# Linear attention on one core: GpSimd adds the seven odd tiles of phi of k, takes relu of k in one piece, and scatters two heads of the output

## The chip, the core and the metric

The kernel runs on one core of a Trainium2 chip. The core has five engines that run beside each other: TensorE (PE in the profile; its weight loads are listed apart as PEld), VectorE (DVE), ScalarE (ACT), GpSimd (POOL) and SyncE (SP, which here only issues transfers). Sixteen DMA engines move data between the chip's memory (HBM) and the core's SBUF. The metric is the time of one execution on the device in microseconds (us); lower is better.

## The reference

The inputs q, k and v have the shape (1, 32, 2048, 128): 32 heads of 2048 rows of 128 numbers in bf16. It is attention without a softmax, so nothing is quadratic in the number of rows.

```python
phi_q = jnp.where(q > 0, q + 1, jnp.exp(q)) + 1e-6
phi_k = jnp.where(k > 0, k + 1, jnp.exp(k)) + 1e-6
kv  = jnp.einsum("bhsd,bhse->bhde", phi_k, v)        # 128 x 128 a head
z   = jnp.einsum("bhsd->bhd", phi_k)                 # column sums
num = jnp.einsum("bhqd,bhde->bhqe", phi_q, kv)
den = jnp.einsum("bhqd,bhd->bhq", phi_q, z)[..., None] + 1e-6
return num / den
```

The kernel uses that phi(x) = min(exp(x), 1) + 1e-6 + relu(x). It never needs the sum of the two parts in one tensor: a matmul with the first part (called `emk` or `emq`) and one with the second (`rk` or `rq`) that accumulate into the same place do the addition. Where the sum is formed first, one matmul takes the place of two.

## The kernel before

**Layout.** A head of q, k, v or the output is 128 partitions of 16 tiles of 128 columns, 4 KB a partition and 512 KB in all. Six buffers each hold heads of k, v and q, ten hold heads of the output.

**What a head goes through.** SP loads k, v and q (L380). ACT makes exp of k (L387). DVE makes `emk` = min(exp, 1) + 1e-6 (L401), 2048 columns at once. POOL makes `rk` = relu of k (L391): heads 0 and 2 in one piece of 2048 columns, head 1 on DVE, heads from 3 on in two halves of 1024. POOL then adds `emk` to `rk` in place for some tiles (L409). PE multiplies these with v (L432) into `kvz_ps`, and for some tiles a matmul of one column with a vector of ones (L339) gives z. For the odd tiles z comes for nothing from a column of ones in v, which POOL writes over the last column of the even tiles of v (memset, L445) once PE has read these. ACT copies `kvz_ps` to SBUF (L449). PE transposes q (L455); ACT makes exp of it (L466) and relu of its second half (L473); DVE makes relu of its first half (L475, source in PSUM) and `emq` (L487), 2048 columns at once. PE makes numerator and denominator of five groups of tiles (L502 with `emq`, L503 with `rq`); DVE adds 1e-6 to the denominators (L525), inverts them (L531) and multiplies (L536 for the last tile, L543 for the rest, in two pieces: groups 0 and 1, then 2 to 4). SP stores the head (L590).

**Which tiles are added.** `ADD` lists the tiles for which POOL forms the sum. For heads from 2 on these are 10 to 14, a block of 640 columns. For the tiles of `ADD`, PE does one matmul; for the others two, one with `emk` and one with `rk`. PE takes the even tiles first, those that need both parts (`both_of`) and then those of `ADD` (`one_of`), in an operation of its own that waits for the add (L442); after that, in the next turn, the odd tiles (`kv2`, L447), which wait for the add and the column of ones.

**Order.** Every operation has a key, and each engine runs its operations in the order of their keys; waits on semaphores follow from what each reads and writes. The keys are heads plus a fraction. On POOL the keys h - 0.45 (first half of relu), h (second half), h + 0.5 (add) and h + 0.6 (memset) give this order:

```
add(h-1), relu(h) first half, memset(h-1), relu(h) second half, add(h), relu(h+1) first half, memset(h), ...
```

The add of head h waits, beside its data, for `emq` of head h - 1 on DVE (`more=`, L421). On DVE a turn is: L525, L531, L536, L543 twice for head n, L475 for n + 2, L401 for n + 3, L487 for n + 2. On PE: num of head n, groups 0 and 1, the odd tiles of n + 1, num of head n, groups 2 to 4, the transposes of n + 2, the even tiles of n + 2.

**Stores.** SP issues all loads and stores in one order; a store's key (`late`, 1 + 1.18 h) puts the later stores behind the last loads. One head, 28, is in `SLOW`: POOL stores it after all its other work with an indirect transfer (L597), a scatter whose row numbers come from seven small DVE instructions at the start (L327 to L334). The row numbers of partitions 16 to 19 and 48 to 51 are out of bounds there, so those rows are left out of the scatter, and SP stores them in four small transfers of 3, 1, 3 and 1 partitions. The last head goes out in two stores.

The functions that the change touches, with the line numbers of the profile:

Of the kernel before, what the change touches and what calls it, by code (L numbers as in the profile page):

```python
# [12 lines left out]
def _ap(base: bass.AP, elem_offset: int, dims):  # L13
    return bass.AP(base.tensor, base.offset + elem_offset, [list(base.ap[0])] + [list(d) for d in dims])
# [217 lines left out]
def bass_standalone__linear_attn_elu__prompt_kernel(  # L232
# [16 lines left out]
    NG = 7  # L249
    HALF = NT * P // 2  # L250
    LAST = NH - 1
    SLOW = {LAST - 3: (16, 48)}

    ADD = (10, 11, 12, 13, 14)
    EVEN, ODD = tuple(range(0, NT, 2)), tuple(range(1, NT, 2))
    MORE = (4, 6, 8, 10, 12, 14)
    GAP = 32
# [7 lines left out]
    with ExitStack() as es:  # L265
        def sb(name, shape, dt):
            return es.enter_context(nc.sbuf_tensor(name, shape, dt))
# [17 lines left out]
        part_sb = sb("part_sb", [P, 1], mybir.dt.int32)  # L285
        off_sb = sb("off_sb", [P, len(SLOW)], fp32)
        num_sb = sb("num_sb", [P, len(SLOW)], fp32)
        row_sb = sb("row_sb", [P, len(SLOW)], mybir.dt.int32)

# [10 lines left out]

        for n, c in (("k", NBI), ("q", NBI), ("v", NBI), ("va", 1), ("o", NBO + 1 + len(SLOW))):
            for i in range(c):
                dsems[(n, i)] = es.enter_context(nc.semaphore(f"s_{n}{i}"))

        pl = Plan()

        def rows(x, h):
# [11 lines left out]
                                                     base=0, pattern=[[-1, P]], channel_multiplier=1),  # L319
               reads=[("id0",)], writes=[("ident",)])  # L320
        pl.add("pool", -7, lambda g: g.memset(_ap(vfull, 0, [[VW, NBI], [1, GAP]]), 1.0), writes=[("vones",)])

        pl.add("pool", -6.9, lambda g: g.iota(part_sb[:], pattern=[[0, 1]], base=0, channel_multiplier=1), writes=[("part",)])
        for i, (h, groups) in enumerate(SLOW.items()):
            off, num, row = off_sb[:, i:i + 1], num_sb[:, i:i + 1], row_sb[:, i:i + 1]
# [12 lines left out]
        def mm_held(pe, out_ap, rhs, stop, start=False):  # L338
            return pe.add_instruction(mybir.InstMatmult(  # L339
                start_tensor_calc=start, stop_tensor_calc=stop, ldweights=False, bass_skip_group_check=True,  # L340
                tile_position=(0, 0), tile_size=(P, P), name=nc.get_next_instruction_name(), engine=mybir.EngineType.PE,
                ins=[pe.lower_ap(rhs), pe.lower_ap(held[0])], outs=[pe.lower_ap(out_ap)]))
# [27 lines left out]
        for h in range(NH):  # L370
            def at(name, key, h=h):
                return place.get((name, h), h + key)

            bi, b2, b3, bo = h % NBI, h % 2, h % 3, h % NBO

            def load(name, buf, src, key, h=h, bi=bi):
                dst, rws = buf[:, bi], rows(src, h)
                if name == "v":
# [9 lines left out]
                   reads=[("k", bi)], writes=[("ek", b2)])  # L388
            def relu_k(eng, key, parts, h=h, bi=bi, b3=b3):
                c = slice(parts[0] * HALF, (parts[-1] + 1) * HALF)  # L390
                pl.add(eng, key, lambda e: e.tensor_scalar(rk_sb[:, b3, c], k_sb[:, bi, c], BIG, 0.0, op0=ALU.min, op1=ALU.max),  # L391
                       reads=[("k", bi)] + ([("rk", h - 1, 1)] if 0 < h < 3 else []),
                       writes=[(n, b3, p) for p in parts for n in ("rk", "rkx")] + [("phik", b3), ("phix", b3)], kind="rk")

            if h < 3:
                relu_k("dve" if h == 1 else "pool", at("rk", 0), (0, 1))
            else:
                relu_k("pool", h - 0.45, (0,))
                relu_k("pool", h, (1,))
            pl.add("dve", at("emk", -3 + 0.95),  # L400
                   lambda d, b2=b2, b3=b3: d.tensor_scalar(emk_sb[:, b3, :], ek_sb[:, b2, :], 1.0, EPS, op0=ALU.min, op1=ALU.add),  # L401
                   reads=[("ek", b2)], writes=[("emk", b3)], kind="emk")

            def add(eng, key, tiles, name, b3=b3, more=()):
                step = tiles[1] - tiles[0]

                def f(e):
                    a, b = (_ap(x[:, :, :], b3 * NT * D + tiles[0] * D, [[step * D, len(tiles)], [1, D]]) for x in (rk_sb, emk_sb))
                    return e.tensor_tensor(out=a, in0=a, in1=b, op=ALU.add)  # L409
                pl.add(eng, key, f, reads=[("emk", b3), ("rkx", b3, 0), ("rkx", b3, 1)] + list(more), writes=[(name, b3)], kind=name)  # L410

            if h == 0:
                add("dve", -2.04, range(NT), "phik")
                both_of, one_of = (), range(NT)
            elif h == 1:
                add("dve", -1.89, MORE, "phix")
                add("dve", -1.88, tuple(j for j in ADD if j in ODD), "phik")
                both_of, one_of = tuple(j for j in EVEN if j not in MORE), MORE
            else:
                add("pool", h + 0.5, ADD, "phik",  # L420
                    more=[("emq", (h - 1) % 3)] + ([("phik", 1)] if h == 2 else []))  # L421
                both_of, one_of = (tuple(j for j in EVEN if (j in ADD) == x) for x in (False, True))

            def kv(pe, tiles, start=False, stop=False, h=h, bi=bi, b3=b3, both_of=both_of):
                for j in tiles:
                    both = j in both_of or (j in ODD and j not in ADD and h > 0)
                    for src in (emk_sb, rk_sb) if both else (rk_sb,):
                        first, fin = start and j == tiles[0] and src is (emk_sb if both else rk_sb), stop and j == tiles[-1] and src is rk_sb
                        w = src[:, b3, j * D:(j + 1) * D]
                        l = j == 0 or (j in ODD and h > 0)  # L430
                        c = GAP + j * D
                        last = pe.matmul(kvz_ps[:, 1 - l:NC], lhsT=w, rhs=v_sb[:, bi, c - l:c + D], start=first, stop=fin,  # L432
                                         skip_group_check=True)
                        if not l:
                            held[0] = w
                            last = mm_held(pe, kvz_ps[:, 0:1], ones_sb[:, 0:1], fin)
                return last
            base = [("v", bi), ("vo", bi), ("ones",), ("vones",)]
            if h:
                pl.add("pe", at("kv", -1.2), lambda pe, kv=kv, t=both_of: kv(pe, t, start=True),  # L440
                       reads=[("emk", b3), ("rk", b3, 0), ("rk", b3, 1)] + base, writes=[("bankkv",)])
            pl.add("pe", at("kv", -1.199), lambda pe, kv=kv, t=one_of, f=h == 0: kv(pe, t, start=f, stop=f),  # L442
                   reads=[("phix" if h == 1 else "phik", b3)] + base + ([] if h else [("first",)]), writes=[("bankkv",)])
            if h:
                pl.add("pool", h + 0.6, lambda g, bi=bi: g.memset(_ap(vfull, bi * VW + GAP + D - 1, [[2 * D, NT // 2], [1, 1]]), 1.0),  # L445
                       reads=[("v", bi)], writes=[("vo", bi)], kind="vo")
                pl.add("pe", at("kv2", -0.2985), lambda pe, kv=kv: kv(pe, ODD, stop=True),  # L447
                       reads=[("phik", b3), ("emk", b3), ("rk", b3, 0), ("rk", b3, 1), ("v", bi), ("vo", bi)], writes=[("bankkv",)])
            pl.add("act", at("kvs", -0.95), lambda a, b3=b3: a.activation(kvs_sb[:, b3, :], kvz_ps[:, 0:NC], ACT.Copy),  # L449
                   reads=[("bankkv",)], writes=[("kvs", b3)], kind="kvs")  # L450
# [31 lines left out]
            else:  # L482
# [5 lines left out]
                   reads=[("eq", b2, 0), ("eq", b2, 1)], writes=[("emq", b3)], kind="emq")  # L488
# [105 lines left out]
            late = h + 1.0 + 0.18 * h  # L594
            if h in SLOW:
                i = list(SLOW).index(h)
# [3 lines left out]
                    reads=[("row", i)] + [("o", bo, p) for p in ("t", 0, 1, 2, 3, 4)], dma=("o", NBO + 1 + i))  # L600
# [38 lines left out]
```

## Time and profile before

| | |
|---|---|
| median of 3 runs | 167.63 us (167.09 to 167.91) |
| the profiled execution: time | 167.01 us |
| the profiled execution: span from first to last instruction | 165.7 us |
| granted clock of TensorE | 1.00 |
| moved by DMA | 67.25 MB, 406 GB/s over the span |
| add on POOL (L409), 640 columns | 30 times, 1397 ns |
| relu on POOL (L391), 1024 columns | 58 times, 1041 ns |
| relu on POOL (L391), 2048 columns | 2 times, 1894 ns |
| emk on DVE (L401) | 32 times, 688 ns |
| emq on DVE (L487) | 32 times, 691 ns |
| scatter on POOL (L597) | once, 1138 ns |

How to read it: the page gives the busy time of each engine as a share of the span, then the span in 40 slices with a digit for the busy tenths, then the chain of work that ended last, followed back from the last instruction. The timeline lists single instructions as start, duration, engine, line, operation, tensors; brackets behind it hold the idle time before it and what ended that. The waits list who waited for whom: total, times, longest. Starts on DVE lie up to 0.09 us before the end of the instruction ahead, since an instruction begins while its forerunner drains; so the price of an instruction is best read from start to start.

### The profile page before, as it was taken

How to read it: one execution, taken by the hardware profiler on the slowest of the kernel's cores; microseconds unless marked ns; L12 is line 12 of the kernel's file. 1: busy time of each engine (PE TensorE's matmuls, PEld its weight loads, DVE VectorE, ACT ScalarE, POOL GpSimd, SP SyncE). 2: the span in 40 equal slices, each digit the busy share in tenths (PEclk: the TensorE clock that was granted, in tenths of full speed). 3: DMA queues.
4: the chain of work that ended last, by engine and by line, in shares of the span. 5: the costliest groups of instructions: out<-in, count | busy, mean ns of one | idle time of the engine just before them, and what ended most of it. 6: DMA issues, size and time to landing. Idle time of an engine off the chain costs nothing.

```text
span 165.7 us, 6280 instructions
## 1 busy us (share of the span) xinstructions
PE 156.2 (94%) x2819; PEld 145.5 (88%) x2453; DVE 153.6 (93%) x277; ACT 155.2 (94%) x143; POOL 107.6 (65%) x130
## 2 busy tenths in 40 slices
PE   7779999999999999999999999999999999999990
PEld 0359899999999999999999989999998999999980
DVE  3587999999999999999999999999999999999993
ACT  3979999999999999999999999999999999999693
POOL 2405787676768867676787767677876767788320
PEclk9999999999999999999999999999999999999999
DMA  5999999999999999999999999999999999999986
GB/s 195 363 419 417 415 415 419 411 411 412 419 420 418 419 419 417 422 418 419 417 421 418 419 420 414 424 416 422 417 421 418 419 419 419 424 415 422 414 344 272
DMA packets 18605, 67.25 MB, mean 406 GB/s; under 512 B 2082, under 2 KB 2210, under 8 KB 18594
## 3 DMA queue, kind: packets, MB, share of 16 engines
q1 hardware_dynamic: 18448, 66.63, 99.2%
q0 software_dynamic: 144, 0.49, 0.7%
q8 instruction: 5, 0.08, 0.2%
q14 instruction: 6, 0.05, 0.1%
q10 hardware_dynamic: 2, 0.00, 0.0%
HBM read 50.33 MB, written 16.81 MB: 405 GB/s over the span
## 4 chain that ended last, share of the span: by engine, by line
DVE 62%; PE 16%; POOL 12%; DMA 4%; issue 3%; ACT 1%; SPq 1%; DVEq 0%
DVE o_sb L543 21%; POOL rk_sb L409 12%; DVE rq_sb L475 12%; DVE emq_sb L487 10%; DVE emk_sb L401 10%; PE kvz_ps L432 6%; PE o_ps L502 5%; PE o_ps L503 5%; DMA k_sb<-in_k_dram 4%; DVE rden_sb L531 3%; DVE o_sb L536 3%; DVE den_sb L525 2%; ACT ek_sb L387 1%; SPq L380 1%; DVE rk_sb L409 0%
## 5 line engine op out<-in xcount | busy, mean ns | idle before, releaser
L432 PE MATMUL kvz_ps<-v_sb,rk_sb 128*128 128x129 bf16 (+1 forms) x512 | 67.0, 220 | 2.7 <-POOL rk_sb L409 0.8
L543 DVE TENSOR_TENSOR o_sb<-o_ps,rden_sb 128x768 bf16<-128x768 f32 (+2 forms) x62 | 67.8, 1134 | 0.0
L409 POOL TENSOR_TENSOR rk_sb<-rk_sb,emk_sb 128x640 bf16<-128x640 bf16 x30 | 41.9, 1397 | 39.4 <-DVE emq_sb L487 38.1
L391 POOL TENSOR_SCALAR rk_sb<-k_sb 128x1024 bf16<-128x1024 bf16 (+1 forms) x60 | 64.2, 1070 | 2.4 <-DMA k_sb<-in_k_dram 2.4
L502 PE MATMUL o_ps<-kvs_sb,emq_sb 128*128 128x129 bf16 (+1 forms) x536 | 65.2, 217 | 0.0
L503 PE MATMUL o_ps<-kvs_sb,rq_sb 128*128 128x129 bf16 (+1 forms) x536 | 64.4, 217 | 0.0
L387 ACT ACTIVATE ek_sb<-k_sb 128x2048 bf16<-128x2048 bf16 x32 | 61.0, 1907 | 2.6 <-DMA k_sb<-in_k_dram 2.6
L466 ACT ACTIVATE eq_sb<-xT_ps 128x2048 bf16<-128x2048 bf16 (+1 forms) x33 | 60.0, 1822 | 2.1 <-PE xT_ps L455 2.1
L432 PE MATMUL kvz_ps<-v_sb,emk_sb 128*128 128x129 bf16 (+1 forms) x338 | 53.3, 221 | 0.5 <-DVE emk_sb L401 0.3
L432 PEld LDWEIGHTS kvz_ps<-v_sb,rk_sb 128*128 128x128 bf16 x512 | 46.1, 98 | 7.5 <-POOL rk_sb L409 2.7
L502 PEld LDWEIGHTS o_ps<-kvs_sb,emq_sb 128*128 128x128 bf16 x536 | 51.2, 98 | 0.8 <-issue 0.5
L503 PEld LDWEIGHTS o_ps<-kvs_sb,rq_sb 128*128 128x128 bf16 x536 | 51.2, 98 | 0.0
L455 PEld LDWEIGHTS xT_ps<-ident,q_sb 128*128 128x128 bf16 x512 | 30.1, 98 | 5.2 <-DMA q_sb<-in_q_dram 4.2
L455 PE MATMUL xT_ps<-ident,q_sb 128*128 128x128 bf16 x512 | 34.0, 220 | 0.7 <-DMA q_sb<-in_q_dram 0.3
L432 PEld LDWEIGHTS kvz_ps<-v_sb,emk_sb 128*128 128x128 bf16 x338 | 32.5, 98 | 0.9 <-DVE emk_sb L401 0.5
L339 PE MATMUL kvz_ps<-ones_sb,rk_sb 128*128 128x1 bf16 x232 | 31.3, 165 | 0.0
L473 ACT ACTIVATE rq_sb<-xT_ps 128x1024 bf16<-128x1024 bf16 x30 | 30.9, 1030 | 0.0
L401 DVE TENSOR_SCALAR emk_sb<-ek_sb 128x2048 bf16<-128x2048 bf16 x32 | 22.0, 688 | 3.6 <-ACT ek_sb L387 3.6
L475 DVE TENSOR_SCALAR rq_sb<-xT_ps 128x1024 bf16<-128x1024 bf16 x34 | 23.2, 688 | 1.0 <-PE o_ps L503 1.0
L487 DVE TENSOR_SCALAR emq_sb<-eq_sb 128x2048 bf16<-128x2048 bf16 x32 | 22.1, 691 | 0.0
L339 PE MATMUL kvz_ps<-ones_sb,emk_sb 128*128 128x1 bf16 x121 | 19.9, 166 | 0.0
L449 ACT ACTIVATE kvs_sb<-kvz_ps 128x129 bf16<-128x129 f32 x32 | 9.0, 282 | 1.5 <-PE kvz_ps L432 0.9
(37 smaller groups left out, 51.6 us busy)
## 6 DMA issues: line engine op xcount, KB each, us to landing
k_sb<-in_k_dram SPq DMA_DIRECT2D x32, 512.0 KB, 14.9
q_sb<-in_q_dram SPq DMA_DIRECT2D x32, 512.0 KB, 15.1
v_sb<-in_v_dram SPq DMA_DIRECT2D x32, 512.0 KB, 15.1
out_dram<-o_sb SPq DMA_DIRECT2D x30, 512.0 KB, 15.3
out_dram<-o_sb SPq DMA_DIRECT2D x1, 288.0 KB, 2.7
out_dram<-o_sb SPq DMA_DIRECT2D x1, 224.0 KB, 2.6
out_dram<-o_sb SPq DMA_DIRECT2D x2, 12.0 KB
out_dram<-o_sb SPq DMA_DIRECT2D x2, 4.0 KB
```

Of the source, the lines that this page charges most:

```text
L339: return pe.add_instruction(mybir.InstMatmult(start_tensor_calc=start, stop_tensor_calc=stop, ldweights=False, bass_skip_group_check=True, ...
L387: lambda a, bi=bi, b2=b2: a.activation(ek_sb[:, b2, :], k_sb[:, bi, :], ACT.Exp),
L391: pl.add(eng, key, lambda e: e.tensor_scalar(rk_sb[:, b3, c], k_sb[:, bi, c], BIG, 0.0, op0=ALU.min, op1=ALU.max), reads=[("k", bi)] + ([( ...
L409: return e.tensor_tensor(out=a, in0=a, in1=b, op=ALU.add)
L432: last = pe.matmul(kvz_ps[:, 1 - l:NC], lhsT=w, rhs=v_sb[:, bi, c - l:c + D], start=first, stop=fin, skip_group_check=True)
L455: last = pe.transpose(xT_ps[:, j * P:(j + 1) * P], q_sb[:, bi, j * P:(j + 1) * P], ident[:])
L466: halves[part] = pl.add("act", key, lambda a: a.activation(eq_sb[:, b2, c], xT_ps[:, c], ACT.Exp), reads=both[part:part + 1] or both, writ ...
L475: f = lambda d: d.tensor_scalar(rq_sb[:, b3, c], xT_ps[:, c], 0.0, None, op0=ALU.max)
L487: lambda d, b2=b2, b3=b3: d.tensor_scalar(emq_sb[:, b3, :], eq_sb[:, b2, :], 1.0, EPS, op0=ALU.min, op1=ALU.add),
L502: pe.matmul(o_ap, lhsT=emq_sb[:, b3, t * P:(t + 1) * P], rhs=kvs_sb[:, b3, c0:c1], start=True, stop=False)
L503: return pe.matmul(o_ap, lhsT=rq_sb[:, b3, t * P:(t + 1) * P], rhs=kvs_sb[:, b3, c0:c1], start=False, stop=True)
L543: pl.add("dve", key, lambda d: d.tensor_tensor(out=o_sb[:, bo, 3 * g0:3 * g1, :].rearrange("p (a b) d -> p a b d", b=3), in0=_ap(full, bas ...
```

## The change

`ADD` becomes the odd tiles 3 to 15, seven tiles with a gap of one tile between them, 896 columns. No even tile is in it, so for heads from 2 on all even tiles take both parts, `one_of` is empty and the operation that waited for the add falls away; of the odd tiles only tile 1 still takes two matmuls. For head 1, whose sums are made on DVE, the add of the odd tiles grows from two tiles (11 and 13) to seven. Relu of k is one instruction of 2048 columns on POOL for heads from 3 on, with the key of the former second half, so that POOL's order becomes

```
add(h-1), memset(h-1), relu(h), add(h), memset(h), relu(h+1), ...
```

And `SLOW` holds heads 27 and 28: both are scattered by POOL at its end, 27 first, each without partitions 16 to 19 and 48 to 51, which SP stores in four small transfers a head; seven more small DVE instructions make the second head's row numbers.

```diff
-    SLOW = {LAST - 3: (16, 48)}
-
-    ADD = (10, 11, 12, 13, 14)
+    SLOW = {LAST - 4: (16, 48), LAST - 3: (16, 48)}
+
+    ADD = (3, 5, 7, 9, 11, 13, 15)
...
             if h < 3:
                 relu_k("dve" if h == 1 else "pool", at("rk", 0), (0, 1))
             else:
-                relu_k("pool", h - 0.45, (0,))
-                relu_k("pool", h, (1,))
+                relu_k("pool", h, (0, 1))
...
                 add("dve", -1.89, MORE, "phix")
-                add("dve", -1.88, tuple(j for j in ADD if j in ODD), "phik")
+                add("dve", -1.88, ADD, "phik")
                 both_of, one_of = tuple(j for j in EVEN if j not in MORE), MORE
             else:
                 add("pool", h + 0.5, ADD, "phik",
                     more=[("emq", (h - 1) % 3)] + ([("phik", 1)] if h == 2 else []))
-                both_of, one_of = (tuple(j for j in EVEN if (j in ADD) == x) for x in (False, True))
+                both_of, one_of = EVEN, ()
...
-            pl.add("pe", at("kv", -1.199), lambda pe, kv=kv, t=one_of, f=h == 0: kv(pe, t, start=f, stop=f),
-                   reads=[("phix" if h == 1 else "phik", b3)] + base + ([] if h else [("first",)]), writes=[("bankkv",)])
+            if one_of:
+                pl.add("pe", at("kv", -1.199), lambda pe, kv=kv, t=one_of, f=h == 0: kv(pe, t, start=f, stop=f),
+                       reads=[("phix" if h == 1 else "phik", b3)] + base + ([] if h else [("first",)]), writes=[("bankkv",)])
```

## The prediction

> **What bounds the kernel now.** I read the page of the profile first: its busy shares, its DMA slices, its chain of work that ended last.
>
> ```profile
> PE 156.2 (94%) x2819; PEld 145.5 (88%) x2453; DVE 153.6 (93%) x277; ACT 155.2 (94%) x143; POOL 107.6 (65%) x130
> ...
> DMA  5999999999999999999999999999999999999986
> ...
> DVE 62%; PE 16%; POOL 12%; DMA 4%; issue 3%; ACT 1%; SPq 1%; DVEq 0%
> ```
>
> The reader is to see four things that are nearly full (PE, DVE, ACT, the DMA engines) and one, POOL, with a third of its time free. The chain runs mostly through DVE; POOL's share of it is one line, the add L409. So a saving on POOL looks cheap and an addition to POOL looks free. The next view, the waits, says what POOL's free time is.
>
> ```profile
> POOL rk_sb L409 <- DVE emq_sb L487: 38.1, 29, 1.5
> ```
>
> Every turn POOL stops for 1.2 to 1.5 us until DVE has ended emq. I therefore took the timeline of POOL and DVE by the turn, a turn running from one start of emq (L487) to the next. From 20.39 us to 153.81 us there are 28 turns, 133.42 / 28 = 4.765 us each. One of them on POOL:
>
> ```profile
> 102.05 1.40 POOL L409 TENSOR_TENSOR rk_sb<-rk_sb,emk_sb 128x640 bf16<-128x640 bf16 x1 [1.23 <-DVE emq_sb L487]
> 103.41 1.04 POOL L391 TENSOR_SCALAR rk_sb<-k_sb 128x1024 bf16<-128x1024 bf16 x1
> 104.39 0.13 POOL L445 MEMSET v_sb<- 128x8 bf16 x1
> 104.46 1.04 POOL L391 TENSOR_SCALAR rk_sb<-k_sb 128x1024 bf16<-128x1024 bf16 x1
> ```
>
> The emq it waited for began at 101.28, so the add begins 0.77 us after emq's start. From start to start the add takes 1.36, the first relu half 0.98, the memset 0.07, and the second half ends at 105.50: 3.45 us of POOL, 4.22 us after emq's start. On DVE the next emk (L401) begins 4.05 us after emq's start in a turn without a wait (20.39 to 24.44, 106.26 to 110.31). So POOL's last relu overlaps the start of emk by up to 0.17 us. What such an overlap costs the start of the kernel shows best, where POOL has a whole relu of 2048 columns:
>
> ```profile
> 13.20 1.89 POOL L391 TENSOR_SCALAR rk_sb<-k_sb 128x2048 bf16<-128x2048 bf16 x1
> ```
> ```profile
> 14.73 0.91 DVE L487 TENSOR_SCALAR emq_sb<-eq_sb 128x2048 bf16<-128x2048 bf16 x1
> 15.56 0.68 DVE L401 TENSOR_SCALAR emk_sb<-ek_sb 128x2048 bf16<-128x2048 bf16 x1
> ```
>
> POOL ends 0.36 us after that emq has begun, and emq takes 0.91 us instead of 0.69: 0.22 us more. In the steady turns:
>
> ```profile
> 80.82 1.04 POOL L391 TENSOR_SCALAR rk_sb<-k_sb 128x1024 bf16<-128x1024 bf16 x1
> ```
> ```profile
> 81.69 0.72 DVE L401 TENSOR_SCALAR emk_sb<-ek_sb 128x2048 bf16<-128x2048 bf16 x1
> 82.33 0.68 DVE L487 TENSOR_SCALAR emq_sb<-eq_sb 128x2048 bf16<-128x2048 bf16 x1
> ```
>
> Here the overlap is 0.17 us, and emq follows emk after 0.64 us instead of 0.60. With an overlap of 0.13 us emk is not longer at all (0.68). All of these fit one rule: **emk and emq (SBUF to SBUF, 2048 columns) do no work until POOL's instruction has ended**; the first 0.135 us of an overlap is start-up and costs nothing, the rest is added whole (0.36 gives 0.22, 0.17 gives 0.04). The halves of rq (L475, from PSUM) lie under the same POOL relu at 13.53 and are not longer (1.29 us for two). So POOL's 3.45 us just fill the room that DVE leaves between emq and the next emk. It is this fit that the change touches.
>
> **The change part by part.**
>
> *The add on POOL* grows from 640 to 896 columns. The row: 1.397 us for 640. POOL's relu gives a fixed part: 2 x 1.04 - 1.89 = 0.19 us. Then (1.397 - 0.19) / 640 = 1.89 ns a column, and 256 columns more are 0.48 us. From above: no fixed part at all, 2.18 ns, 0.56 us, plus 0.03 for seven pieces with gaps (the memset L445 of 8 strided columns takes 0.135, those of one column about 0.10). From below: a fixed part of 0.29, a whole small POOL instruction (L318, 128 columns), gives 1.73 ns and 0.44 us. I take 0.48; DVE's rows for pieces with gaps (256 columns 0.286 us, 768 in 0.559, 2048 in one piece 1.224) lie on one line, which speaks for no price of the gaps. The Trainium skill's page "GPSIMD Engine Reference", section "Elementwise — side-by-side cycle accounting", gives about 2.6 cycles an element for such an add at 1.2 GHz; by that 256 columns would be 0.55 us and the sum further down would come out 2 us higher (an estimate from that page).
>
> *The relu in one piece* is 1.89 instead of 0.98 + 1.04, so POOL from add to relu's end is (1.36 + 0.48) + 0.07 + 1.89 = 3.80 us instead of 3.45.
>
> *The turn that follows.* POOL ends 0.77 + 3.80 = 4.57 us after emq's start; emk begins at 4.05 and overlaps by 0.52; it is lengthened by 0.52 - 0.135 = 0.385. Behind emk on DVE stands emq, and behind emq POOL's next add (it waits for emq), so the delay closes into a loop: 4.05 + 0.385 + 0.60 = 5.035 us a turn, whatever PE and ACT do. That is 0.27 more than 4.765, and 28 turns make **+7.56 us**. The first relu of this kind adds its own: the add of head 2 starts at 16.33, its memset waits for PE until about 18.35, relu ends near 20.3, emk begins at 19.79: 0.39 us before the first turn. The rows reach only to an overlap of 0.36; 0.52 is taken on the same line. The Trainium skill's page "SBUF — State Buffer", section "SBUF: two separate sides", speaks against the change here: GpSimd and a VectorE instruction in a two-port mode share one port pair that the first takes for its whole instruction while the other fully blocks. By that the line goes on to any overlap, as I have it; the sum stands on the rows alone.
>
> *PE.* In start-to-start times of the trace a matmul of 128 or 129 columns is 57 ns, one of a single column (L339) 27 ns. A head's kv goes from 27 and 11 of them to 25 and 14: 33 ns less. The even pass grows from 1.04 to 1.29 us and no longer waits for the add; the odd pass falls from 0.81 to 0.51. PE's work is near 4.56 us a head, 0.47 below the new turn, so its waits on POOL (L432, some 0.17 us a head) vanish without showing.
>
> *The memset L445* comes straight after the add now and waits for the even pass of PE. PE starts a head's num when the first division ends (2.3 us after emq's start) and needs 0.82 + 0.57 + 1.02 + 0.90 + 1.29 until the even pass ends: 2.1 us into the next turn. The add ends at 2.61. Half a microsecond of cover; the price without it is a rival.
>
> *Start.* Seven more index instructions on DVE (0.19 us each from start to start) follow 2.93 us, where DVE idles until 6.01: nothing, 1.3 us without that cover. The add of head 1 on DVE goes from 0.29 to 0.63 us at 12.29; DVE waits for PE until 13.53, and PE's odd pass reads it at 13.74: nothing, 0.34 without cover.
>
> *Stores.* Head 27 leaves SP's queue as one store of 512 KB and comes back as four small ones, 1.2 us of issue. Behind them stand the stores of 29 to 31, the first of which waited 4 us for DVE: nothing, else up to 1.2. POOL gets one more scatter of 1.14 us behind its last memset, with nothing queued behind it. The first scatter went out 3.60 us after the last emq's start and landed 5.9 us later. With the last turn at 153.81 + 7.95 = 161.76, the second goes out near 166.5 and lands by 172.4, a microsecond before the end.
>
> *The end.* The last store is issued at 163.08, its sixteen completions come from 164.96 to 165.68. The latest completion of the stores of 27, 29, 30 and 31 comes at 161.82, 163.11, 164.41, 165.16, 165.68, each behind the other by the time of its own bytes: one DMA engine that never runs dry. Eight microseconds later the backlog is gone; I take 0.3 off (between 0 and 0.7, the spread of the sixteen).
>
> Sum: 7.56 + 0.39 - 0.3 = **+7.65 us**. Against the profiled execution, span 165.7 and 167.01 us in all, that is 173.4 and 174.7. The median of the runs shown is 167.63, 0.62 above it; on that I forecast **175.3 us**.
>
> **The rivals.**
>
> *Not slower: the block does not grow.* If an overlap past 0.36 us costs emk nothing further because POOL gives way, and DVE hides what is left, the turn falls to DVE's own 4.67, since PE no longer waits for the add. That takes 28 x 0.09 = 2.5 us off the computing, but the DMA engines then set the end: without head 27 on the slowest, the next one ended at 165.37, 0.3 to 0.5 below. 167.2 on the median. It decides from a lengthening of emk below 0.11 us (4.05 + 0.60 + 0.11 = 4.76). For it: that 0.52 is beyond the rows. Against: two overlaps on one line. Chance 0.09.
>
> *The block stops at what was seen*, 0.22 us: turn 4.87, 28 x 0.105 + 0.1, 170.7. Chance 0.05.
>
> *The memset waits for PE.* If PE comes 0.8 us later than worked out, relu starts 0.3 us later every turn: 8 us more, 183.5. For it: the even pass is 0.25 us longer, and the last memset did wait 0.58. Against: PE gains 0.47 of slack a turn. Chance 0.07.
>
> **How the numbers follow.** Forecast 0.79; the add's bounds of 0.44 and 0.59 move the turn by -0.04 and +0.11, the sum by -1.1 and +3.1, 174.2 to 178.4. The range reaches down through half of the way to the smaller block and up a little: 171.5 to 179. Over and under 0.5% (0.84 us, about what a measurement of this kernel can tell): slower 0.91; the first rival is mostly within, 0.06, faster 0.03.
>
> **What would show it.** Right: emk's mean rises from 688 ns to about 1070, emq and den stay, the relu is 1.89 and the add 1.88 us, the turn 5.03, POOL's wait for emq 1.2 us a turn, DMA slices below full. Wrong: emk still at 0.7 us; an add far from 1.9; waits of L445 on PE in every turn; a last landing that is a scatter's.

## The result, and the profile after

The changed kernel takes 174.62 us (median of 6 runs, 173.49 to 175.21); the kernel before, run beside it, 167.53 us (167.09 to 167.91). The ratio is 1.0417, 95% interval 1.038 to 1.0454: slower. The forecast was 175.3 us in a range of 171.5 to 179.

The page of the changed kernel, the lines that answer to those of before:

```profile
PE 154.3 (89%) x2844; PEld 143.1 (82%) x2388; DVE 162.6 (94%) x284; ACT 156.3 (90%) x143; POOL 118.8 (68%) x102
...
DMA  5999999999999999999999999999999999992095
...
DVE 77%; issue 12%; DMA 4%; PE 3%; ACT 1%; SPq 1%; DVEq 0%
```

DVE keeps its share though its list of work has hardly grown: its busy time rose by 9 us. POOL has left the chain that ended last, and the DMA engines, full to the end before, are nearly idle from about 158 to 165 us. The waits of the changed kernel (total, times, longest):

```profile
POOL rk_sb L408 <- DVE emq_sb L487: 35.7, 29, 1.2
PEld o_ps L502 <- DVE o_sb L543: 14.9, 30, 0.5
```

POOL still waits for emq once a turn, and PE now waits once a turn for DVE's division, which it did not before. One turn on POOL (timeline of the changed kernel; its lines stand one lower than before from L401 to L432, the others where they were):

```profile
101.48 1.88 POOL L408 TENSOR_TENSOR rk_sb<-rk_sb,emk_sb 128x896 bf16<-128x896 bf16 x1 [1.23 <-DVE emq_sb L487]
103.30 0.13 POOL L445 MEMSET v_sb<- 128x8 bf16 x1
103.37 1.89 POOL L391 TENSOR_SCALAR rk_sb<-k_sb 128x2048 bf16<-128x2048 bf16 x1
106.49 1.88 POOL L408 TENSOR_TENSOR rk_sb<-rk_sb,emk_sb 128x896 bf16<-128x896 bf16 x1 [1.23 <-DVE emq_sb L487]
```

and beside it on DVE:

```profile
104.76 1.05 DVE L400 TENSOR_SCALAR emk_sb<-ek_sb 128x2048 bf16<-128x2048 bf16 x1
105.73 0.68 DVE L487 TENSOR_SCALAR emq_sb<-eq_sb 128x2048 bf16<-128x2048 bf16 x1
```

Relu ends at 105.26, 0.50 us after emk has begun, and emk takes 1.05 us. Every one of the 28 turns from 20.51 to 160.86 us is 5.01 to 5.02 us long; before they alternated between 4.69 and 4.79, every sixth 4.97 to 4.99.

The difference of the two profiled spans, 8.2 us, falls into four parts: the turns, 28 x (5.0125 - 4.765) = 6.9; the first full turn, which begins 0.1 later; the stretch from the last emq of a full turn to the issue of the last store, 9.76 instead of 9.27, 0.5; and from that issue to the last landing, 3.23 instead of 2.60, 0.6. The medians differ by less, 7.1 us, which the turns and the first turn (7.0) all but make up: the profiled execution of the changed kernel, 175.21 us, was the slowest of its six, so what its trace shows at the end is probably more than the median holds.

### The profile page after: what moved, and what is told of

Read it like the earlier page. It is cut to its first block, busy times and chain, and to the rows that moved or that the text cites. A ratio compares the mean times of both kernels' runs of the same rounds, so it can differ in the third digit from the quotient of the medians.

```text
span 173.9 us, 6198 instructions
## 1 busy us (share of the span) xinstructions
PE 154.3 (89%) x2844; PEld 143.1 (82%) x2388; DVE 162.6 (94%) x284; ACT 156.3 (90%) x143; POOL 118.8 (68%) x102
## 4 chain that ended last, share of the span: by engine, by line
DVE 77%; issue 12%; DMA 4%; PE 3%; ACT 1%; SPq 1%; DVEq 0%
DVE o_sb L543 25%; DVE emk_sb L400 17%; DVE rq_sb L475 12%; DVE emq_sb L487 10%; DVE rden_sb L531 5%; DVE o_sb L536 5%; DMA k_sb<-in_k_dram 4%; DVE den_sb L525 2%; PE o_ps L503 1%; ACT ek_sb L387 1%; PE o_ps L502 1%; SPq L380 1%; PE kvz_ps L431 1%; DVE rk_sb L408 0%; DVEq L220 0%
## 5 line engine op out<-in xcount | busy, mean ns | idle before, releaser
L408 POOL TENSOR_TENSOR rk_sb<-rk_sb,emk_sb 128x896 bf16<-128x896 bf16 x30 | 56.3, 1878 | 36.9 <-DVE emq_sb L487 35.7
L431 PE MATMUL kvz_ps<-v_sb,rk_sb 128*128 128x129 bf16 (+1 forms) x512 | 62.0, 220 | 0.9 <-DVE rk_sb L408 0.9
L391 POOL TENSOR_SCALAR rk_sb<-k_sb 128x2048 bf16<-128x2048 bf16 x31 | 58.7, 1893 | 2.5 <-DMA k_sb<-in_k_dram 2.5
L431 PE MATMUL kvz_ps<-v_sb,emk_sb 128*128 128x128 bf16 (+1 forms) x273 | 46.6, 218 | 0.7 <-issue 0.4
L431 PEld LDWEIGHTS kvz_ps<-v_sb,rk_sb 128*128 128x128 bf16 x512 | 40.7, 98 | 2.5 <-DVE rk_sb L408 2.0
L339 PE MATMUL kvz_ps<-ones_sb,rk_sb 128*128 128x1 bf16 x232 | 36.4, 165 | 0.0
L339 PE MATMUL kvz_ps<-ones_sb,emk_sb 128*128 128x1 bf16 x211 | 34.6, 166 | 0.0
L400 DVE TENSOR_SCALAR emk_sb<-ek_sb 128x2048 bf16<-128x2048 bf16 x32 | 32.2, 1007 | 2.3 <-ACT ek_sb L387 2.3
L431 PEld LDWEIGHTS kvz_ps<-v_sb,emk_sb 128*128 128x128 bf16 x273 | 26.4, 97 | 1.1 <-DVE emk_sb L400 1.1
```

What stands on the lines that cost most here:

```text
L339: return pe.add_instruction(mybir.InstMatmult(start_tensor_calc=start, stop_tensor_calc=stop, ldweights=False, bass_skip_group_check=True, ...
```

## The experiments

Three theories were on trial. **Blocking**: emk on DVE does no work until POOL's instruction has ended, so that POOL's work from the end of emq to the end of relu sets the turn. **PE**: its new order (all even tiles in one long pass) sets it. **Scatter**: the second scatter at the end brought the time. Each run below is compared with the kernel before on the same chip; "overlap" is from emk's start to the end of POOL's instruction.

**Fewer tiles in the add.** The changed kernel with six odd tiles, then with five:

```diff
-    ADD = (3, 5, 7, 9, 11, 13, 15)
+    ADD = (5, 7, 9, 11, 13, 15)
```

> The changed kernel with six odd tiles (5 to 15, 768 columns) in the add instead of seven; nothing else is changed. Blocking theory (emk on DVE does no work until POOL's relu has ended): the add falls from 1.878 us by 128 x 1.88 ns to 1.64, POOL ends 0.24 us sooner after emq's start, emk overlaps relu by 0.26 instead of 0.50 us and takes about 0.80 us instead of 1.04; the turn is 5.01 - 0.24 = 4.77 us, near the 4.765 of the kernel before, so that the time falls by 28 x 0.24 = 6.7 us to about 168. PE theory (the new order on PE, an even pass of 30 matmuls, sets the turn): the even pass is the same and one more tile needs two matmuls, the turn stays at 5.0 to 5.07 and the time at 174.6 or a little over. Scatter theory (the second scatter at the end brought the time): no change, 174.6.

Measured: 167.88 us, ratio 1.0014 (0.9986 to 1.0042). Add 1.637 us, turn 4.77 us in all 28, emk from the timeline:

```profile
62.74 0.81 DVE L400 TENSOR_SCALAR emk_sb<-ek_sb 128x2048 bf16<-128x2048 bf16 x1
63.46 0.68 DVE L487 TENSOR_SCALAR emq_sb<-eq_sb 128x2048 bf16<-128x2048 bf16 x1
```

0.24 us off the add is 0.24 us off every turn, with PE's order and both scatters left in place. That rules out the PE and the scatter theory for the bulk of the time.

```diff
-    ADD = (3, 5, 7, 9, 11, 13, 15)
+    ADD = (7, 9, 11, 13, 15)
```

> The changed kernel with five odd tiles (7 to 15, 640 columns, as many as before the change). Blocking theory: the add takes 1.40 us, POOL's relu ends 0.48 us sooner than with seven, 4.07 us after emq's start, 0.02 after emk's start, so emk takes 0.68 us as without POOL. The turn is no longer set by POOL but by DVE (4.65) or PE (4.59 us of matmuls before, plus 3 x 27 ns: 4.67), and the DMA engines are full again to the end: 166.5 to 167.5 us, no slower than the kernel before. PE theory: the even pass of 30 matmuls stays and two more odd tiles need two matmuls each, turn 5.0 to 5.1, 174.6 to 177. Scatter theory: 174.6.

Measured: 168.18 us, ratio 1.0036 (1.0008 to 1.0064); the 166.5 to 167.5 expected was missed. The turns alternate between 4.65 and 4.93 us, mean 4.79. The waits, and two turns on POOL's timeline:

```profile
POOL v_sb L445 <- PE kvz_ps L339: 12.2, 16, 7.1
```
```profile
51.66 1.89 POOL L391 TENSOR_SCALAR rk_sb<-k_sb 128x2048 bf16<-128x2048 bf16 x1
54.79 1.40 POOL L408 TENSOR_TENSOR rk_sb<-rk_sb,emk_sb 128x640 bf16<-128x640 bf16 x1 [1.23 <-DVE emq_sb L487]
56.50 0.13 POOL L445 MEMSET v_sb<- 128x8 bf16 x1 [0.32 <-PE kvz_ps L339]
56.57 1.89 POOL L391 TENSOR_SCALAR rk_sb<-k_sb 128x2048 bf16<-128x2048 bf16 x1
```

With the add this short the memset is the one that waits, for PE's even pass, in every other turn; relu starts 0.3 us later than the add allows, and emk is held again (about 0.95 us in those turns, 0.70 in the others). This is the third rival of the prediction, which the longer add hides.

**One scatter, two scatters.** The changed kernel with head 28 alone in `SLOW`, and the kernel before with both heads:

```diff
-    SLOW = {LAST - 4: (16, 48), LAST - 3: (16, 48)}
+    SLOW = {LAST - 3: (16, 48)}
```

> The changed kernel with head 28 alone scattered and head 27 stored by SP in one store, as before the change. Blocking theory: the turns stay at 5.01 us and the last store is issued at the same time (170.6 in the profiled execution); the DMA engines stand idle before the last stores, so one head more or less on the slowest engine does nothing there, but the 1.3 us of transfers of head 27's scatter no longer lie ahead of the last stores: 0 to 0.7 us less, 173.9 to 174.6. Scatter theory: back to 167.5.

Measured: 174.12 us, ratio 1.038 (1.0336 to 1.0424). Turn 5.01 us. The last store goes out 9.27 us after the last emq of a full turn, as before the change, and lands 2.11 us later.

```diff
-    SLOW = {LAST - 3: (16, 48)}
+    SLOW = {LAST - 4: (16, 48), LAST - 3: (16, 48)}
```

> The kernel before with heads 27 and 28 both scattered; nothing else of the change. Blocking theory: the turns stay at 4.765 us, emk at 0.69. At the end of the kernel before one DMA engine never ran dry and landed last, 0.3 us behind the next; it loses head 27's eight packets of 0.16 us: 0 to 0.5 us less, 167.0 to 167.5. If the second scatter comes too late instead (its packets start about 1.1 us after the first one's), its bytes lie in front of the last three stores: up to 0.6 us more, 168.1. Scatter theory: 174.6.

Measured: 168.0 us, ratio 1.0024 (0.9998 to 1.005). Neither gain nor loss is shown by the interval; the gain of 0 to 0.5 us that the blocking theory expected did not come. The last store goes out 10.42 us after that emq instead of 9.27, but lands 2.1 us later instead of 2.6; the last landing is at 166.71 us, where it was at 165.68.

**Relu whole, add as before.** The kernel before with two scatters and relu in one piece:

```diff
-                relu_k("pool", h - 0.45, (0,))
-                relu_k("pool", h, (1,))
+                relu_k("pool", h, (0, 1))
```

> The kernel before with two of the three edits: relu of k in one piece and two scatters, but the add over tiles 10 to 14 as before, so that the even tiles 10, 12, 14 again wait for the add on PE. Blocking theory: POOL's own work is shorter than before the change (1.36 + 0.07 + 1.89 = 3.32 us), but the memset between add and relu must now wait for PE's even pass, whose last six matmuls begin only when the add has ended (2.2 us after emq's start) and end 0.45 us later; the former first half of relu lay in that gap. Relu then starts 2.8 us after emq's start and ends at 4.69, emk overlaps it by 0.64 and takes about 1.19 us, the turn is 5.16 us, the time 167.5 + 28 x 0.4 = 178.5 us with the second scatter. A theory that counts only POOL's or the add's length (640 columns, no more work than before) expects 167.5 to 168. PE theory: the even pass is that of before, 167.5.

Measured: 177.07 us, ratio 1.0568 (1.0507 to 1.0628); turn 5.11 us, slower than the changed kernel, with less work on POOL than it (106.0 us busy against 118.8) and than the kernel before (107.6). Waits and POOL's timeline (in this kernel all lines after 400 stand one lower):

```profile
POOL v_sb L444 <- PE kvz_ps L339: 23.1, 31, 7.2
```
```profile
93.04 1.39 POOL L408 TENSOR_TENSOR rk_sb<-rk_sb,emk_sb 128x640 bf16<-128x640 bf16 x1 [1.23 <-DVE emq_sb L486]
94.95 0.13 POOL L444 MEMSET v_sb<- 128x8 bf16 x1 [0.52 <-PE kvz_ps L339]
95.02 1.89 POOL L391 TENSOR_SCALAR rk_sb<-k_sb 128x2048 bf16<-128x2048 bf16 x1
```

The half of relu that used to lie between add and memset covered PE's last six matmuls, which wait for the add. Taken away, it leaves POOL idle 0.52 to 0.58 us every turn, and relu ends later, not sooner.

**Relu in halves, add over seven tiles.** The changed kernel:

```diff
-                relu_k("pool", h, (0, 1))
+                relu_k("pool", h - 0.45, (0,))
+                relu_k("pool", h, (1,))
```

> The changed kernel with relu of k in two halves again, in the old order (first half between add and memset); the add over the seven odd tiles stays. Blocking theory: POOL from the add to the end of the second half takes 1.84 + 0.98 + 0.07 + 1.04 = 3.93 us instead of 3.80; emk overlaps the second half by 0.64 us, takes 1.19 us, and the turn is 5.01 + 0.14 = 5.15 us: 28 x 0.14 = 4 us more, 178.5 us. If only the length of the single instruction that emk meets counted (1.04 instead of 1.89 us), the turn would fall, towards 4.8 us and 168.

Measured: 178.55 us, ratio 1.0659 (1.0602 to 1.0715); turn 5.16 us. Its emk (on L401 in this kernel):

```profile
96.35 1.19 DVE L401 TENSOR_SCALAR emk_sb<-ek_sb 128x2048 bf16<-128x2048 bf16 x1
```

What counts is when POOL's chain ends, not how long the instruction is that emk meets: emk meets one of 1.04 us and is held longer than by one of 1.89.

**Without the wait for emq.** The changed kernel:

```diff
-                    more=[("emq", (h - 1) % 3)] + ([("phik", 1)] if h == 2 else []))
+                    more=[("phik", 1)] if h == 2 else [])
```

> The changed kernel without the add's wait for emq; the add still waits for emk and relu of its own head. Blocking theory with the port going to whoever comes first: emq follows emk on DVE at once, the add needs about 0.08 us for its semaphore, so emq comes first, the add is held until emq ends and starts without a semaphore's delay: add's duration 2.3 to 2.5 us, turn 4.93 to 4.98 us, 1 to 2 us less, 173 us. If POOL gets the port first instead: emq is held for the whole add (emq's duration 2.4 us and more), the turn is 6.5 us or more and the time over 210. Without any blocking in this direction: the add runs beside emq, starts 0.6 us sooner and emk is hardly blocked, turn 4.7 us and 167.

Measured: 168.08 us, ratio 1.004 (1.0014 to 1.0066); turn 4.79 us, where 4.93 to 4.98 was expected. DVE, then POOL:

```profile
93.01 0.68 DVE L487 TENSOR_SCALAR emq_sb<-eq_sb 128x2048 bf16<-128x2048 bf16 x1
```
```profile
93.17 2.26 POOL L408 TENSOR_TENSOR rk_sb<-rk_sb,emk_sb 128x896 bf16<-128x896 bf16 x1 [0.63 <-DVE emk_sb L400]
```

emq came first and was not lengthened; the add, 1.88 us elsewhere, took 2.26. The reading that fits is that emq held POOL, as relu holds emk, but only until 93.17 + 2.26 - 1.88 = 93.55, 0.54 us after its start and 0.14 before its recorded end. (In the runs without the wait further down, adds of 640 and 768 columns are longer by the same 0.37 us.) The wait on the semaphore starts the add 0.76 us after emq's start; being held instead is 0.22 us cheaper a turn. The expectation had put the release at emq's recorded end.

**The first scatter earlier.** The changed kernel, with head 27's scatter ahead of the last add:

```diff
-                pl.add("pool", LAST + 0.65 + 0.01 * i, lambda g, bo=bo, i=i: g.indirect_dma_start(
+                pl.add("pool", LAST + (0.65 if h == LAST - 3 else 0.45), lambda g, bo=bo, i=i: g.indirect_dma_start(
```

> The changed kernel with the scatter of head 27 before the last add instead of after the last memset, into POOL's last wait for emq (1.2 us; the scatter takes 1.14). In the changed kernel the second scatter runs 4.33 to 5.49 us after the last emq of a full turn, DVE's next instruction after the final emq starts 0.4 us after that scatter's end, 0.5 us later than with one scatter, and the last store is issued 9.76 instead of 9.27 us after that emq. If the second scatter is what holds the tail: 9.27 again, 174.1 us as with one scatter. If the transfers of head 27 do it: no change, 174.6. If the early scatter overlaps emk and emq and holds them as relu does: up to 1 us more, 175.6.

Measured: 173.74 us, ratio 1.038 (1.0332 to 1.0428). DVE's end in the changed kernel, and then here:

```profile
165.54 0.68 DVE L487 TENSOR_SCALAR emq_sb<-eq_sb 128x2048 bf16<-128x2048 bf16 x1
166.78 0.17 DVE L525 TENSOR_SCALAR den_sb<-o_ps 128x12 f32<-128x12 f32 x1 [0.56 <-PE o_ps L503]
```
```profile
165.40 0.68 DVE L487 TENSOR_SCALAR emq_sb<-eq_sb 128x2048 bf16<-128x2048 bf16 x1
166.00 0.16 DVE L525 TENSOR_SCALAR den_sb<-o_ps 128x12 f32<-128x12 f32 x1
```

The 0.56 us wait is gone and the last store goes out 9.22 us after the last emq of a full turn. That the place of the second scatter makes the wait is not shown by this. Seven of the profiled kernels issue the second scatter directly behind the first. In four DVE waits there: 0.56 us in the changed kernel, 0.76 with six tiles, 0.71 with five, 1.20 in the kernel before with two scatters. In the other three (relu whole with the add as before, relu in halves, no wait for emq) it does not. The last of these, POOL and then DVE:

```profile
159.82 0.98 POOL L597 DMA_INDIRECT out_dram<-o_sb,row_sb  x1 [0.30 <-issue]
```
```profile
159.94 0.68 DVE L487 TENSOR_SCALAR emq_sb<-eq_sb 128x2048 bf16<-128x2048 bf16 x1
160.54 0.16 DVE L525 TENSOR_SCALAR den_sb<-o_ps 128x12 f32<-128x12 f32 x1
```

In these three the last store goes out at 9.22 us, as here, but lands 3.13 us later instead of 2.15. So, where the DMA engines had run dry before, a second scatter directly behind the first goes with a later end in single traces: the last landing comes 12.4 to 13.0 us after the last emq of a full turn in three (the changed kernel, relu whole, relu in halves), and 11.4 us in two (one scatter, and this run). Whether the issue or the landing is late differs from trace to trace. By the times alone (intervals 1.038 to 1.0454 and 1.0332 to 1.0428) no gain of this run is shown.

**Versions that might beat both.** Six odd tiles, no wait for emq, one scatter; the same with five; and the kernel before without the wait for emq:

```diff
-    SLOW = {LAST - 4: (16, 48), LAST - 3: (16, 48)}
-    ADD = (3, 5, 7, 9, 11, 13, 15)
+    SLOW = {LAST - 3: (16, 48)}
+    ADD = (5, 7, 9, 11, 13, 15)
...
-                    more=[("emq", (h - 1) % 3)] + ([("phik", 1)] if h == 2 else []))
+                    more=[("phik", 1)] if h == 2 else [])
```

> The changed kernel with six odd tiles (5 to 15), without the add's wait for emq, and with head 28 alone scattered. Blocking theory: from the run without that wait (turn 4.79 with seven tiles, emk overlapped by 0.27) 0.24 us of add are taken away, so relu ends 0.03 us after emk's start and emk is not held: 0.68 us. The turn falls to DVE's 4.65 or to PE's work of some 4.6 us, unless the memset waits for PE's even pass, as it did with five tiles (12.2 us in all). The DMA engines then set the end: 166.5 to 167.3 us, 0 to 0.5% below the kernel before. If the lost wait changes which of emq and the add goes first, the turn is 6 us and the time over 200.

Measured: 167.19 us, ratio 0.9983 (0.9957 to 1.0008). The turns alternate between about 4.67 and 4.85, mean 4.76: the memset waits for PE in every other one, as with five tiles, so the 4.65 expected was missed.

> The same with five odd tiles (7 to 15). Blocking theory: POOL has 0.24 us more room, which the memset cannot use: it comes sooner but waits for PE's even pass, which ends where it did. emk is held in every other turn as in the run with five tiles and the wait (4.65 and 4.93 us in turn, mean 4.79): 167.2 to 168 us, no better than with six.

Measured: 167.63 us, ratio 1.0014 (0.999 to 1.0039), turn 4.79, as expected. For the third the edit is the `more=` line alone, in the kernel before.

> The kernel before with one edit: the add does not wait for emq. Blocking theory: emq holds the add until about 0.54 us after its start instead of the 0.77 of the wait, so POOL's second half of relu ends 0.22 us sooner, before emk starts, and PE's last even tiles get their sum 0.22 us sooner; PE's waits for POOL (0.17 us a head) go, the turn falls from 4.765 to 4.65 to 4.69 us, 2 to 3 us less of computing, of which the DMA engines leave at most 0.5: 166.7 to 167.4 us.

Measured: 167.22 us, ratio 0.9991 (0.9963 to 1.002). The turn falls to 4.67 and the last store is issued at 160.80 us instead of 163.08, 2.3 us sooner; yet it lands at 165.86, where 165.68 was the last landing before. The DMA slices of this run's page:

```profile
DMA  5999999999999999999999999999999999999994
```

Full from the first microseconds to the end: a faster turn is worth nothing here, since 67 MB have to pass. No version tried is faster than the kernel before beyond its interval.

## Why the prediction was right, point by point

*The fit of POOL's work between emq and the next emk* was what the change touched, and it decided. The rule "the first 0.135 us of an overlap is free, the rest is added whole" was read from overlaps of 0.17 and 0.36 us. emk without a block takes 0.68; the runs give, as overlap and lengthening: 0.26 and 0.12 (six tiles), 0.50 and 0.365 (seven), 0.59 and 0.46 (relu whole, old add). All lie on the line; 0.365 and 0.46 lie past the 0.22 us at which the second rival let the block stop. This agrees with the Trainium skill, page "SBUF — State Buffer", section "SBUF: two separate sides", which says that GpSimd and a two-port VectorE instruction exclude each other for a whole instruction; the run without the wait shows the other direction of it, POOL held by emq, though only until 0.14 us before emq's recorded end.

*The add* was put at 1.36 + 0.48 us from start to start; it is 1.82, and 1.878 in itself: 1.88 ns a column for the 256 added, from 1.397 and 1.637 for 640 and 768 the same. The gaps between the tiles cost nothing: 640 columns take 1.397 us in one block and 1.395 as five tiles with gaps. The 2.6 cycles of the Trainium skill's page "GPSIMD Engine Reference", section "Elementwise — side-by-side cycle accounting", which stand there for fp32, are 2.17 ns at 1.2 GHz (an estimate from that page), too many for this add in bf16; the measurement decides.

*The turn*: 5.035 forecast, 5.0125 measured; 6.9 us in 28 turns instead of 7.56. The small difference is three hundredths in POOL's chain (4.54 us after emq's start instead of 4.57), of which 0.02 go into every turn. emk takes 1.04 us in these turns, where about 1.07 was forecast.

*The first block* was put at 0.39 us; emk of the first turn meets relu for 0.38, not 0.52, and this turn began 0.13 us sooner, so 0.1 is left. Mis-sized by 0.27.

*PE*: its waits on POOL (2.7 us in all on L432) are gone without a gain, as forecast; it waits for DVE instead.

*The memset* had half a microsecond of cover, and waits nowhere in the changed kernel but at the start. Its rival was rightly priced low for this change: with the add cut to five tiles the cover is gone, as that run shows.

*The end* was the weak step. "With nothing queued behind it" was true of the second scatter on POOL, and still 0.5 us was lost in the profiled execution, through a wait of DVE for PE that no row of before showed and that three of seven kernels with such a scatter do not have. And the 0.3 us taken off the last landing was right in size for the runs with one late scatter (issue to last landing 2.11 and 2.15 instead of 2.60), but the profiled run of the changed kernel has 3.23: the trace lists one packet of 4 KB at 165.70 us that took 1.68 us where the others take 0.16, and the last of the sixteen completions of each of the last six stores, the two scatters among them, comes 1.2 to 1.8 us after the others. The packet alone does not explain that: the two runs with one late scatter have one too (0.82 and 1.22 us), and their last three stores are not late. What delays the end stays open. The sum was +7.65; the profiled spans differ by 8.2, the medians by 7.1. That the sum came so near is in part luck: the turns and the first block were put 0.9 us too high, and the end 1.4 us too low by the traces (0.4 by the medians).

*The range.* Its lower bound, 171.5, is below what the rule beside it gives (half of the way from 174.2 down to 170.7 is 172.4); the measured time lies above both.

*The first rival* (not slower) held that without the block the DMA engines set the end. The block did grow; but the other half of that rival is shown by the kernel before without the wait: 2.3 us of computing saved, nothing gained.

## What to carry to other kernels

An engine that is idle for a third of the time has no free time if its idle stretch is the one in which another engine's instruction would hold it or be held by it: lay the two timelines over each other before adding work to it, and look for single instructions of one shape with two durations. Where an operation is split in two, ask what lies between the halves; here the first half covered a wait of the instruction behind it. And before a stage is made faster, see whether the transfers leave room for the gain.

## What was not expected of the hardware

A two-input add of GpSimd that is held by VectorE's emq gets going, by its length, 0.54 us after emq's start, 0.14 us before emq's recorded end, so that being held is cheaper than waiting for its semaphore (0.76 us).

A scatter does not hold VectorE as relu does: emq takes 0.68 us at 165.54 although the second scatter runs from 165.18 to 166.34, and 0.68 us at 160.72 in the run with the early scatter, which runs from 160.43 to 161.81. What is late beside the second scatter in the changed kernel is PE's signal: the trace's semaphore events show PE's increments for three matmuls that ended at 165.02, 165.36 and 165.70 only at 166.6 to 166.8. In the four kernels with this wait DVE's next instruction starts 0.3 to 0.6 us after the scatter's end. In the three others whose second scatter follows directly on the first, it starts while the scatter still runs, so the scatter alone does not delay PE's increments. What does is left open; no run separates the causes.
